# One fused recurrent-attention and feed-forward kernel: another written-out order of its steps

## The chip, the cores and the metric

The kernel runs on one core of a Trainium2 chip. The metric is the time of one execution on the device in microseconds (us); lower is better. The five engines of a core are called PE (matrix multiply; its weight loads are listed as PEld), DVE (vector), ACT (activations), POOL (general purpose) and SP, which here only issues transfers (DMAs).

## The reference

What is computed is a gated recurrent attention (an mLSTM) whose output goes through a gated feed-forward layer, all in float32:

```
q, k, v, o_gate: (4, 8, 768, 40);  i_gate, f_gate: (4, 8, 768)
for t in range(768):
    m_new = max(f[t] + m, i[t])
    C = exp(f[t] + m - m_new) * C + exp(i[t] - m_new) * outer(v[t], k[t])
    n = exp(f[t] + m - m_new) * n + exp(i[t] - m_new) * k[t]
    y[t] = sigmoid(o_gate[t]) * (C @ q[t]) / max(abs(n . q[t]), 1)
x = y as (3072, 320)
out = (sigmoid(x @ w_gate) * (x @ w_val)) @ w_out        # w_gate, w_val: 320x1536, w_out: 1536x320
```

## The kernel before

The sequence is cut into 6 chunks of 128 positions; with 4 batch entries that makes 24 units (chunk, batch entry), numbered 0 to 23, four to a chunk. Within a unit the recurrence is a masked matrix product: the scores (keys against queries) are multiplied by a matrix of decays and then applied to the values; between chunks a small state is carried.

The feed-forward layer works on whole chunks (512 rows of x). A chunk has 12 columns of blocks of the hidden width, and the first blocks are split in two halves, so that there are 103 feed-forward tiles, numbered 0 to 102; tiles 0 to 15 are chunk 0. Every product is made from a high and a low part of each operand, so a tile has 16 accumulating matmuls up (steps `t0` to `t102`, line L950), a tanh on ACT (`ta`, L963), a gate multiply on DVE (`tg`, L966), a split into a high (`th`) and a low part (`tl`, L977) and matmuls down (`p`, L988). PE, DVE, ACT and POOL each run their own instructions in the order in which they were issued.

Weights arrive in double words of 8 bytes and are decoded on the chip: for each of 30 pieces of weight, step `w..a` is an ACT operation, `w..b` three DVE operations in a row (L529, L533, L537), `w..d` the high part, `w..e` the low part (L578, L582, L584), `w..f` the load of a later piece into the freed buffer. `wg`, `wv` and `wr` are the first three pieces, `w3` to `w29` the rest. All pieces are needed by the tiles of chunk 0.

The order of all this is not computed in the kernel. It is a string, ORDER, of some 4,470 words. Each word names a list of prepared operations; each time the word comes up, the next operation of its list is issued, and `*3` issues three. A `/` issues nothing and only switches which of two PSUM buffers (the matrix unit's result memory) the next small result takes:

```
for word in ORDER.split():
    if word == "/":
        other("pa")
        continue
    key, _, n = word.partition("*")
    for _ in range(int(n or 1)):
        f, args = todo[key].pop(0)
        f(*args)
```

The opening computes units 0 and 1 by special steps. `ig`, `ih`, `iac` and `gc`, `g` are scans and small operations on the gates (DVE, L1178); `sp` spreads the gates on PE and `ex` takes the exponential on ACT; `mk` masks on POOL; `tr` transposes keys and queries on PE (L644, L647), `cp` copies them out (on DVE and ACT); `sc` makes scores on PE (L1104), `ti` multiplies them by the decays (DVE, L1109); `c0`, `c1` apply them to the values (PE, L759); `cv`, `cg`, `cr`, `cx` normalise and gate (DVE); `d0`, `d1` transpose the result on PE (L886), `dx`, `dy` write its high and low part as the feed-forward operand. Later units have `a`, `ah`, `b`, `bm`, `c`, `ci`, `cf`, `cs`, `cv`, `cg`, `cr`, `cx`, `d`, `dx`, `dy` for the same stages, and `z`, `zd`, `za`, `zm`, `zs` for the carried state. In the opening the second transposed block of unit 1 (`tr12`) takes the PSUM buffer that the scores `sc01` held, so it has to wait until `ti01` has read them. `lq`, `lk`, `lv`, `lo` and `ld` are loads issued by SP. `im` and `iq` are matmuls on zeros that keep PE at work.

Of the kernel before, what the change touches and what calls it, by code (L numbers as in the profile page):

```python
# [153 lines left out]
cv7 p16 t17*2 as8.5 t17 as8.7 t17 p15*2 t17 p15 oh1 as8.6 t17*2 cv6 t17*2 ta17 t17 p16*2 a10.0 cg6 p15*3 as8.4 t18
p16*2 cr6 aq8*2 t18*3 tg17 t18 cv7 th17 a11.0 t18*2 za6 p16 ld10 t18 ct8 o0 cx6 t18*4 p17 ah10.0 s8 p17 t18*3 tl17 e9a
p17 p15 t18 ta18 tg18 p15 d6 dx6 cg7 za7 p15 t19*3 th18 s8 t19*6 p17 t19*2 dy6 t19*3 p18 t19*2 / ci8 tl18 p17 p18 cv7
s8 cr7 ta19 s8 p18 tg19 t20*4 p17 t20*2 as9.1 t20 cf8 e8m cx7 t20 th19 as9.2 t20 tl19 t20 p19 t20*2 ah11.0 v9 t20*4
p19 p18 b8.2 p18 ta20 p19 p18 t21 tg20 t21*3 p19 bk8 th20 t21 b8.1 t21*3 bm8.2 as9.0 b8.0 t21*4 tl20 t21*2 o1 as9.3
# [1049 lines left out]
```

## Time and profile before

| | us |
|---|---|
| median of three runs | 522.29 (521.57 to 522.36) |
| the profiled execution, its time | 521.88 |
| the profiled execution, its span (first to last instruction) | 520.2 |
| around the span | 1.68 |
| PE busy | 502.3 |
| DVE busy | 318.8 |
| ACT busy | 191.1 |
| POOL busy | 156.8 |

The span is read with the engines' busy times: PE is busy for 97% of it. The mean granted clock of PE was 0.997 of full speed.

### The profile page before, as it was taken

How to read it: one execution, taken by the hardware profiler on the slowest of the kernel's cores; microseconds unless marked ns; L12 is line 12 of the kernel's file. 1: busy time of each engine (PE TensorE's matmuls, PEld its weight loads, DVE VectorE, ACT ScalarE, POOL GpSimd, SP SyncE). 2: the span in 40 equal slices, each digit the busy share in tenths (PEclk: the TensorE clock that was granted, in tenths of full speed). 3: DMA queues.
4: the chain of work that ended last, by engine and by line, in shares of the span. 5: the costliest groups of instructions: out<-in, count | busy, mean ns of one | idle time of the engine just before them, and what ended most of it. 6: DMA issues, size and time to landing. Idle time of an engine off the chain costs nothing.

```text
span 520.2 us, 13187 instructions
## 1 busy us (share of the span) xinstructions
PE 502.3 (97%) x5191; PEld 453.6 (87%) x5191; DVE 318.8 (61%) x738; ACT 191.1 (37%) x483; POOL 156.8 (30%) x207
## 2 busy tenths in 40 slices
PE   8699999999999999999999999999999999999997
PEld 7577887777899999998888888888888888999997
DVE  7899999998745657755456743847625444443322
ACT  4586667456223332233314223122323224122221
POOL 3546333445435320342402143213041321101111
PEclk9899999999999999999999999999999999999999
DMA  9777949778777995868979797498786687000000
GB/s 204 172 202 208 245 116 252 181 160 149 171 148 127 206 217 106 179 146 183 158 161 173 162 199 155 117 183 166 135 186 156 126 177 158 23 7 2 27 25 26
DMA packets 234382, 76.66 MB, mean 147 GB/s; under 512 B 213840, under 2 KB 222224, under 8 KB 234320
## 3 DMA queue, kind: packets, MB, share of 16 engines
q1 hardware_dynamic: 233232, 75.56, 67.1%
q8 instruction: 41, 0.67, 0.6%
q10 hardware_dynamic: 1088, 0.26, 0.3%
q14 instruction: 21, 0.17, 0.1%
HBM read 57.61 MB, written 17.14 MB: 144 GB/s over the span
## 4 chain that ended last, share of the span: by engine, by line
PE 82%; DVE 11%; issue 2%; ACT 1%; DMA 1%; POOL 1%; SPq 0%; DVEq 0%; POOLq 0%
PE pg L950 47%; PE po L988 23%; PE av L759 3%; PE s L781 2%; PE in L802 2%; DVE dc L537 1%; PE xt L886 1%; DVE gl L977 1%; PE s L776 1%; DVE dc L529 1%; PE av L627 1%; DMA st_o<-in_moe_w_out_dram 1%; DVE sg L966 1%; DVE xl L899 1%; DMA gin<-in_f_gate_dram 1%
## 5 line engine op out<-in xcount | busy, mean ns | idle before, releaser
L963 ACT ACTIVATE sg<-pg 128x256 f32<-128x256 f32 (+1 forms) x103 | 48.2, 468 | 231.4 <-PE pg L950 211.0
L966 DVE SCALAR_TENSOR_TENSOR sg<-sg,pg 128x256 f32<-128x256 f32 (+1 forms) x103 | 54.0, 525 | 109.3 <-ACT sg L963 65.2
L950 PE MATMUL pg<-xl,wh 128*128 128x256 f32 (+1 forms) x412 | 108.8, 330 | 0.2
L950 PE MATMUL pg<-xh,wh 128*128 128x256 f32 (+1 forms) x412 | 107.6, 333 | 1.0 <-ACT sg L963 0.6
L950 PE MATMUL pg<-xh,wl 128*128 128x256 f32 (+1 forms) x412 | 108.0, 331 | 0.0
L977 POOL TENSOR_TENSOR gl<-sg,gh 128x256 fp32r<-128x256 f32 (+1 forms) x51 | 48.8, 958 | 196.1 <-ACT gh L971 63.1
L988 PE MATMUL po<-oh,gl 128*128 128x320 f32 x288 | 88.0, 315 | 1.3 <-DVE gl L977 1.1
L988 PE MATMUL po<-oh,gh 128*128 128x320 f32 x288 | 87.9, 316 | 0.6 <-DVE gh L973 0.6
L988 PE MATMUL po<-ol,gh 128*128 128x320 f32 x288 | 88.2, 315 | 0.0
L950 PEld LDWEIGHTS pg<-xl,wh 128*128 128x128 f32 x412 | 69.8, 189 | 5.5 <-DVE xl L899 0.6
L950 PEld LDWEIGHTS pg<-xh,wh 128*128 128x128 f32 x412 | 69.2, 189 | 5.9 <-ACT sg L963 1.6
L950 PEld LDWEIGHTS pg<-xh,wl 128*128 128x128 f32 x412 | 69.3, 188 | 5.7 <-DVE wl L578 0.5
L950 PE MATMUL pg<-xl,w 128*128 128x256 f32 (+1 forms) x206 | 61.5, 335 | 0.0
L988 PEld LDWEIGHTS po<-oh,gl 128*128 128x128 f32 x288 | 53.7, 188 | 5.7 <-DVE gl L977 1.9
L988 PEld LDWEIGHTS po<-oh,gh 128*128 128x128 f32 x288 | 53.6, 188 | 5.5 <-DVE gh L973 1.3
L988 PEld LDWEIGHTS po<-ol,gh 128*128 128x128 f32 x288 | 53.7, 189 | 3.4
L950 PE MATMUL pg<-xh,w 128*128 128x256 f32 (+1 forms) x206 | 53.6, 330 | 0.0
L787 DVE TENSOR_TENSOR d<-s,d 128x384 f32<-128x384 f32 (+1 forms) x66 | 32.6, 506 | 25.9 <-PE s L781 20.8
L971 ACT ACTIVATE gh<-sg 128x256 fp32r<-128x256 f32 (+1 forms) x58 | 28.9, 498 | 48.3 <-DVE sg L966 32.6
L479 ACT ACTIVATE d<-d,at 128x128 f32<-128x128 f32 x136 | 42.7, 390 | 3.7 <-DMA d<-mscr 3.7
L977 DVE TENSOR_TENSOR gl<-sg,gh 128x256 fp32r<-128x256 f32 (+1 forms) x52 | 32.2, 619 | 14.4 <-ACT gh L971 7.0
L950 PEld LDWEIGHTS pg<-xl,w 128*128 128x128 f32 x206 | 36.6, 189 | 2.6
(151 smaller groups left out, 686.5 us busy)
## 6 DMA issues: line engine op xcount, KB each, us to landing
d<-mscr SPq DMA_DIRECT2D x22, 512.0 KB
k<-in_k_dram SPq DMA_DIRECT2D x24, 160.0 KB
v<-in_v_dram SPq DMA_DIRECT2D x24, 160.0 KB
o<-in_o_gate_dram SPq DMA_DIRECT2D x24, 160.0 KB
st_o<-in_moe_w_out_dram SPq DMA_DIRECT2D x12, 320.0 KB
scr0q<-qt SPq DMA_DIRECT2D x32, 120.0 KB
...
```

Source lines behind the costliest of these rows:

```text
L479: nc.scalar.activation(d[:, h, :], d[:, h, :], AF.Exp, bias=at[:, c, b * H + h : b * H + h + 1], scale=-1.0)
L529: nc.vector.tensor_scalar(t, t, MAX_POS, MAX_NEG, ALU.min, ALU.max)
L759: nc.tensor.matmul(dst[xs], lhs[:, xs], rhs, start=True, stop=True)
L781: nc.tensor.matmul(ps[g][:, m, :], ks[: 3 * D, h0 + m, :], qs[: 3 * D, h0 + m, :], start=True, stop=True)
L787: nc.vector.tensor_tensor(x, ps[g][:, :nh, :], x, ALU.mult)
L802: nc.tensor.matmul(pi[:, h0 : h0 + nh, :], qk[u][:r, g, :], cb[:r, b // 2, g, b % 2, : nh * DA], start=True, stop=True)
L950: nc.tensor.matmul(pg[x], w[:, a, fs] if a < 2 else w[:, fs], y[c][:, a, n0:n1], start=first, stop=a == 2 and y is xl)
L963: nc.scalar.activation(sg[0], pg[0], AF.Tanh, scale=0.5)
L966: nc.vector.scalar_tensor_tensor(sg[0], sg[0], 1.0, pg[1], ALU.add, ALU.mult)
L971: nc.scalar.activation(gh[u][:, :nt], sg[0], AF.Copy)
L977: E('gl0' if c == 0 else 'gl', f'tl{n}').tensor_tensor(gl[u][:, :nt], sg[0], gh[u][:, :nt].bitcast(F32), ALU.subtract)
L988: nc.tensor.matmul(po[t], g[c, j, t0][:, (t - t0) * P : (t - t0 + 1) * P], o[:, j, :], start=j == 0 and first, stop=j == NF - 1 and last)
```

## The change

Only the string ORDER differs. The same words stand in it, each as often as before, apart from the `/`, of which there are 43 in place of 37. So every operation, its operands, its engine and its size stay; what moves is the order in which each engine is given its instructions and SP its transfers, and which of two PSUM buffers some of the small results take. The first 165 steps follow an older sequence, and all behind them is laid anew. The first 21 words agree. Shown are the opening up to tile 0, and the stretch around tile 14 and 15:

```
     'PU': 4,
 }
 ORDER = """
-w26f w25f w29f w28f w21f iw ip*2 it if ii lq0 lk0 ib x0 x1 v1 lk1 lq1 iy ig ir x2 ig im ia gc*2 ig ih ig ih lv1 is im
-sp00 sp01 iac tr01 tr02 cp02 tr00 ex01 cp01 ex00 g wva wga cp00 wvb*2 wgb igs sc01 im tr10 tr11 v0 gc*2 cp11 lo1 sc02
-lq2 cp10 lv0 wvb wra sp10 ex10 g wgb g wgb sc00 sp11 sc11 mk01 mk00 wrb lo0 bk0 wrb*2 ti01 x4 ex11 mk11 tr12 sc10 wgd
-cp12 ti00 mk10 wvd ti02 bk1 wve ti10 c0 ie sc12 iq cv0*2 lk2 ld2 ct0 ti12 ti11 w3a z1 cv0 c1 a2.1 cg0 wrd cr0 zm1 cx0
-cv1 ct1 wge d0 w3b cv1 w3b ah2.1 w3b cv1 cg1 cr1 g w3d x3 dx0 dy0 e2 cx1 im d1 iq dx1 a2.0 w5a t0*2 dy1 t0 g lk3 t0
-ah2.0 lq3 z0 a3.0 v2 e2a t0*2 w5b*3 ah3.0 t0*3 zm0 w3f t0*2 g w5d w5e wre t0*3 wgf wrf ld3 w7a t0 ta0 a2.2 ah2.2 t0
...
-ta14 lv7 tg14 lq11 w28d aq8 e8a th14 t15 ct7 p13*3 w29b t15 tl14 t15 cf7 p13 w29b p13 t15*6 v8 p14 w28e t15*3 aq7.1
-t15*3 lv8 ta15 e7m bk7 b7.1 t15 p13*2 p14 t16 ct6 tg15 p14 lk8 t16*2 bm7.1 as9.6 zd8 t16*2 p13 e8 t16*3 p14 cs6 / b7.2
-p14 aq7.0 t16 p14 a8.1 p14 th15 lo8 t16 v7 t16*2 w29d zd6 tl15 ah8.1 w29e t16*2 p14 t16 p14 as9.5 p15 ta16 as9.7 bm7.2
...
+w26f w25f w29f w28f w21f iw ip*2 it if ii lq0 lk0 ib x0 x1 v1 lk1 lq1 iy ig v0 ig im ia ir is ig im ih igs iac ih x2
+gc sp00 gc g ex00 lv0 sp01 lo1 tr01 ig ex01 g mk00 tr02 lo0 tr00 cp01 wga mk01 cp02 sc01 cp00 wgb bk0 wva im tr10 wgb
+tr11 x4 cp10 sc02 wgb lv1 wra sp10 cp11 wvb lk2 ti01 ex10 sc00 wvb lq2 wrb sp11 wrb ex11 gc mk10 sc11 wrb ti00 tr12
+sc10 ti02 mk11 cp12 ld2 wvb wgd x3 c0 bk1 w3f ct0 ct1 sc12 cv0 cg0 wrd wge iq ti12 z1 wvd cv0 ti10 lk3 ti11 c1 wve zm1
+lq3 cv0 cr0 w3a a2.1 cx0 v2 cv1 wre cg1 d0 wgf ah2.1 cv1 w3b dx0 cv1 cr1 e2 ld3 w3b cx1 im d1 w3b gc dy0 iq w3d wrf g
+dx1 lv2 a2.0 w3e w5a dy1 w7a g t0 w5b ah2.0 t0 lq4 t0 w5b t0 e2a t0 z0 w7b g t0 a2.2 w5b w7b zm0 e2m ah2.2 gs a3.1 w5d
+lo2 t0*3 ah3.1 t0 zi t0 h0 t0*2 h0c t0*3 b2.0 ta0 w6a tg0 a3.0 w5e th0 bk2 ah3.0 e3a p0*2 t1*2 w6b t1*3 gs v5 w7b /
...
+ah7.1 w28b ta14 w28b w29b a7.0 w28d lk8 aq7.1 p13 t14 ah9.1 cs6 t15 ct6 p12 al9.1 tg14 t15*3 bk7 t15 as9.4 t15 th14
+t15 aq8 aq7.2 t15*2 ld9 tl14 za6 t15 cg6 t15 as9.7 t15 cv6 p13 aq8 t15 p13 w28e lv8 t15 v8 t15 w29b p13 as9.5 p13 w29b
+ta15 p13*2 a8.1 p13 ah7.0 p13 p14*2 w29d t15 cv6 ah8.1 t16 cv6 t16 w29e tg15 t16*2 p14 t16 p14 p13 al8.1 / ci7 th15
+p13 e8 p14 cf7 as8.6 p14 tl15 t16*2 cr6 t16 as8.5 p14 t16 a9.0 p14 t16 lo10 p14 t16*2 aq7.0 as8.4 t16 ah9.0 / b7.2
...
```

## Rows read from the trace of the kernel before

**Rows 1.** The page's part on busy time, share of the span and instructions.

```profile
PE 502.3 (97%) x5191; PEld 453.6 (87%) x5191; DVE 318.8 (61%) x738; ACT 191.1 (37%) x483; POOL 156.8 (30%) x207
```

**Rows 2.** Stretches: length, busy (instructions) by engine, PE's clock, DMA share, GB/s.

```profile
28.50:114.00 85.50, 80.50 (x856) 67.43 (x857) 81.75 (x189) 56.34 (x149) 38.65 (x45) 1.00 0.76 192
114.00:150.00 36.00, 34.56 (x405) 31.17 (x404) 25.55 (x56) 13.56 (x38) 16.91 (x23) 1.00 0.79 162
150.00:500.00 350.00, 349.12 (x3542) 321.22 (x3541) 185.22 (x427) 100.87 (x244) 86.04 (x108) 1.00 0.67 138
500.00:520.20 20.20, 16.84 (x131) 16.56 (x129) 4.56 (x12) 4.02 (x10) 2.93 (x4) 1.00 0.09 33
```

**Rows 3.** The same columns for two stretches of the opening.

```profile
10.00:20.00 10.00, 6.75 (x96) 4.85 (x94) 9.04 (x18) 7.02 (x19) 4.64 (x6) 0.95 0.99 226
20.00:30.00 10.00, 8.27 (x181) 6.76 (x174) 7.66 (x24) 7.17 (x19) 4.79 (x8) 0.88 0.59 155
```

**Rows 4.** PE's longest wait in the first 30 us: in total, times, longest.

```profile
PE pt L644 <- DVE d L1109: 2.9, 1, 2.9
```

**Rows 5.** DVE in order of time, opening: start, us, instruction, idle before it.

```profile
8.08 1.15 DVE L664 COPY kq<-pt 80x384 f32<-80x384 f32 x2 [1.77 <-PE pt L647]
...
12.95 0.15 DVE L1178 TENSOR_TENSOR mend<-gin,mg 32x1 f32<-32x1 f32 x1
13.03 0.67 DVE L537 SCALAR_TENSOR_TENSOR dc<-st,dc 128x512 int32<-128x512 int32 x1
...
14.57 0.47 DVE L1178 TENSOR_TENSOR_SCAN mg<-gin,mend 32x128 f32<-32x128 f32 x1
...
17.28 1.35 DVE L1109 TENSOR_TENSOR d<-s,d 128x384 f32<-128x384 f32 x3
```

**Rows 6.** PE in order of time, from the second unit's scores to tile 0.

```profile
14.10 0.91 PE L1104 MATMUL s<-kq 120*128 120x384 f32 x2 [0.39 <-ACT d L1084]
17.88 0.31 PE L644 MATMUL pt<-ident,k 128*80 128x128 f32 x1 [2.87 <-DVE d L1109]
...
18.24 0.81 PE L1104 MATMUL s<-kq 120*128 120x384 f32 x2
18.98 1.28 PE L759 MATMUL av<-v,d 128*32 128x41 f32 x64
...
22.33 0.88 PE L759 MATMUL av<-v,d 128*32 128x41 f32 x64
...
27.97 0.50 PE L950 MATMUL pg<-xh,wh 128*128 128x256 f32 x2
```

**Rows 7.** DVE in order of time, ahead of tile 0.

```profile
24.43 0.49 DVE L537 SCALAR_TENSOR_TENSOR dc<-st_o,dc 128x320 int32<-128x320 int32 x1
...
25.98 0.46 DVE L1178 TENSOR_TENSOR mend<-gin,mg 32x1 f32<-32x1 f32 x1
26.37 0.54 DVE L899 TENSOR_TENSOR xl<-xt,xh 128x384 fp32r<-128x384 f32 x1
26.83 0.17 DVE L869 COPY x<-x 128x64 f32<-128x64 f32 x1
```

**Rows 8.** ACT in order of time, the high part of weight piece 3.

```profile
24.96 0.47 ACT L562 ACTIVATE oh<-dc 128x320 fp32r<-128x320 f32 x1 [0.53 <-DVE dc L537]
```

**Rows 9.** DVE in order of time, around the gate multiply of tile 15.

```profile
127.12 0.69 DVE L966 SCALAR_TENSOR_TENSOR sg<-sg,pg 128x512 f32<-128x512 f32 x1 [0.34 <-PE pg L950]
...
128.60 0.79 DVE L698 STREAM_TRANSPOSE kr<-k 128x320 f32<-128x320 f32 x1
```

**Rows 10.** DVE groups by shape from 28 to 114 us: busy, mean ns, idle before.

```profile
L537 DVE SCALAR_TENSOR_TENSOR dc<-st,dc 128x512 int32<-128x512 int32 x10 | 8.4, 842 | 0.1
```

**Rows 11.** Line 537 in the whole span: min/median/max ns, first and last start.

```profile
L537 DVE SCALAR_TENSOR_TENSOR dc<-st,dc x18: 406/676/1705, 13.0 to 112.2; 128x512 int32<-128x512 int32 x12, 128x256 int32<-128x256 int32 x6
```

**Rows 12.** DVE and POOL in order of time, around 88 us.

```profile
87.71 1.71 DVE L537 SCALAR_TENSOR_TENSOR dc<-st,dc 128x512 int32<-128x512 int32 x1
...
87.58 1.29 POOL L977 TENSOR_TENSOR gl<-sg,gh 128x512 fp32r<-128x512 f32 x1 [6.87 <-ACT gh L971]
```

More of the change, by code (lines that the diff above doesn't have):

```diff
@@ L154 @@
[L154 to L158, printed above, removed]
@@ new lines @@
+lo3 p0 t2*2 w4b t2 gcs t2 e3m tg1 t2 b2.2 ah3.2 w8a p0 ct2 t2*2 w4b b3.1 bk3 bm2.2 w4d w7f t2 lk4 th1 c2 w6e w5f v3
+w8b tl1 t2 cv2 bm3.1 t2*4 cv2 ld4 t2 cg2 w4e t2 b3.0 cv2 ta2 cr2 ct3 t3 w8b t3 t2 w9a b3.2 w8b t3 w9b p1 w8d w8f t3
+bm3.2 t3*2 p1 bm3.0 w8e p1 / z2 tg2 c3 w9b th2 cx2 w9b zm2 tl2 t3 cv3 t3 w11a w9f t3 cv3 cg3 t3 d2 wvf w9d cv3 p1 p2
+cr3 w6f dx2 t3*3 w11b t3 zs1 t3 cx3 t3 p2 w11b ta3 p2 d3 w9e dy2 lk6 p1*2 dx3 tg3 p2 zs1 gc z3 th3 w12a t4 lq5 tl3 t4
+dy3 zm3 t4 p2 e4 t4 p3 w12b p3 v4 g p2 w11b / k0 t4 a4.2 t4 w13a w12b t4*2 g t4 k0c t4 ah4.2 t4 lq6 w12b t4*3 aq4.2 t4
@@ new lines @@
+dx6 ld10 t17 t18 s8 t18 tg17 t18 p16 al10.0 s8 p15 dy6 t18*2 as9.1 t18 p16 cs7 p15 s8 p15 t18 cv7 oh1 t18 za7 p15 t18
+th17 ct7 t18 o1 t18 tl17 t18*2 lk10 t18 cg7 t18 p16*2 ta18 t18 lo9 p16 oh3 p16 tg18 p17 t19*3 th18 t19*2 p17 tl18
+t19*3 a11.0 t19*3 p17 t19*2 cv7 t19 cv7 t19 p17*2 ta19 p18*3 t19 p17 t20 tg19 p18*2 cr7 p18 t20*3 th19 t20*2 tl19
+t20*3 as10.1 p19 t20*2 e10a t20 aq9 t20*3 zs7 ci8 ta20 t20 b8.1 o3 tg20 t21*2 zs7 bm8.1 t21 e10 t21 p19*2 th20 t21*2
+a10.1 aq9 t21 tl20 t21*2 as10.2 t21*4 ah10.1 t21 cf8 t21*2 al10.1 / b8.0 ta21 p20 e9 p19 bm8.0 p19 cx7 t22 as10.4 p20
@@ new lines @@
+v10 tg21 t22 p19 t22 ah11.0 t22 th21 b8.2 e9m t22*2 s9 bm8.2 t22*2 p20 aq9 p21 t22*2 zd8 as10.0 t22*3 tl21 p20 s9 t22
+p20 t22 s9 t22 d7 zd9 s9 ta22 c8 oh2 zs7 e10m tg22 dx7 ct8 dy7 as10.5 ct10 t23 v11 t23 cs8 p21 lk11 th22 t23*2 p20
+as10.7 cv8 t23 p21 cv8 tl22 t23*2 cv8 t23*4 al11.0 t23 p22 t23*4 p21 ta23 p21*2 p22 tg23 p22 t24*3 th23 as10.3 t24*4
+tl23 t24*5 p22 t24 as11.3 p23 t24*2 ci9 ta24 o2 t24 as11.0 p22 t25 tg24 t25 p22 lv10 t25 a11.1 t25 th24 t25*4 tl24 t25
+cf9 t25 aq10 t25*2 cg8 t25 ld11 t25*3 cr8 p23 as10.6 ta25 p23 p24 ah11.1 p23 tg25 aq10 p23*2 bk9 t26 lq15 th25 t26*3
@@ new lines @@
+t39*5 e13a t39 aq12 t39*3 s12 t39*3 s12 t39*3 s12 / d10 ta39 aq12 c11 dx10 as13.1 lo12 cs11 t40 p37 tg39 lk14 t40*3
+th39 t40*3 tl39 t40*3 cv11 t40 dy10 t40*2 p38 za11 p38*2 cg11 t40*2 p39 t40 ta40 p39*2 p38 tg40 p38 t41*2 a15.0 t41
+th40 t41*2 p38 t41 cv11 t41 tl40 t41 cv11 t41*2 cr11 t41*2 zs9 p40 v15 t41 cx11 t41*2 d11 ld14 ta41 t41 p39*2 tg41
+aq12 p39 t42*2 oh7 t42*3 th41 t42 o7 t42*2 oh6 p40 tl41 zs9 t42 dx11 t42*2 p40 e13 p41 dy11 t42 aq13 p40 p41 t42 aq13
+t42*3 aq13 p40 ta42 p40 b12.0 as13.4 tg42 b12.2 p41 bm12.0 zs11 t43 th42 t43*2 ct14 t43*2 tl42 t43 ah15.0 t43 lv15
@@ new lines @@
+a14.1 t43*4 al15.0 o6 t43*2 p42 t43*2 p42 p41 ta43 p41 p42 e14 b12.1 t43 p41 s13 t44 tg43 p42 s13 t44*2 ah14.1 t44 s13
+t44 bm12.1 t44 al14.1 t44 s13 t44*3 zs11 t44*2 th43 t44*3 tl43 t44 p42 as14.5 / ci12 ta44 lo13 p43 p42 tg44 p43*2
+a14.0 p43 th44 p43*2 ct12 t45*2 bm12.2 t45*3 tl44 t45*3 ah14.0 t45*3 al14.0 t45*3 p44 t45*2 e13m c12 ta45 tg45 cf12
+th45 zd13 t46 lk15 cs12 t46 zd12 t46 as14.3 t46*2 as14.0 t46 ci13 as15.1 t46 cf13 t46 p44 tl45 p44 lv14 p44 t46 cv12*2
+t46 cv12 t46 cg12 as14.1 t46 p45 cr12 t46*2 as14.7 bk13 t46*2 as14.2 ta46 p44 p45 p44 / b13.0 e14a p45 as14.4 t47
@@ new lines @@
+ah16.1 p47*2 t49 p48*2 tg49 t50*3 cv13 th49 p48 t50 dx12 t50*2 cr13 t50 as15.6 t50 al16.1 t50 dy12 t50 p48 as15.7 p48
+tl49 p48 p49 t50 aq15 t50 as16.5 t50*2 as16.4 t50 zd14 p49*2 ta50 zd15 aq15 / b14.2 t50 lo15 bm14.2 p48 p49 tg50 p48
+b14.0 p48 t51 th50 b14.1 t51 e16a s15 bm14.1 t51*2 s15 bm14.0 t51 s15 t51 cx13 t51 lo16 e16 tl50 p49 / d13 zs13 c14
+dx13 e16m s15 dy13 lq18 t51 a16.0 p50*2 p49 bk16 p49 p50 p49*2 zs13 ah16.0 p50 v18 t51*6 ld18 t51 p49 zs13 ci14 ta51
+ct15 t51 p50 p49 tg51 p50*2 t52*2 th51 t52 al16.0 t52*2 cf14 t52 as16.2 t52 cs14 t52 as16.6 p49 t52 za14 as16.7 p50
@@ new lines @@
+tl51 t52*2 lk17 cg14 p51 t52*4 p50 t52 as16.0 zd16 ta52 / ci15 lq21 p51*2 cf15 t53*2 cv14 tg52 p50 as17.3 p50*2 p51
+cv14 t53 th52 cv14 t53 as16.3 cr14 / b15.2 t53*2 as16.1 t53 b15.1 p51*2 bm15.1 p51*2 t53 tl52 t53 / b15.0 bm15.2 p51
+t53 s16 cx14 bm15.0 t53 lv16 p51*2 t53 as17.1 t53*3 p52 d14 ta53 c15 e18 cs15 t53 lk18 p52 cv15 za15 p52 zs13 p52 cv15
+cg15 p52*2 t54 cv15 p52 cr15 s16 t54 p52 s16 tg53 p51 cx15 t54 s16 v19 t54*2 zs15 th53 t54 / d15 tl53 t54 aq16 dx15
+t54 aq16 t54 dx14 t54 aq16 t54 a18.0 p52 as17.0 t54*2 ld17 t54 ah18.0 t54 a17.1 p53 al18.0 p53 ta54 p52*2 p53 dy14
@@ new lines @@
+e18a tg57 t58*3 p55 p56 p55 t58 p55*3 t58 as18.7 th57 t58 za16 t58 tl57 cf16 t58 p56 a19.0 t58*4 ah19.0 t58 cs16 p57
+lv17 p57 t58*3 lk19 ta58 p56*2 p57*2 ct17 p57 tg58 p57 ct16 aq18 p56*3 aq18 p57 th58 t59 lv18 t59 cv16 tl58 cv16 t59
+cg16 aq18 t59 p57*2 t59*2 e18m t59 p58*2 p57 t59*2 zd18 p58*2 t59 / b17.0 t59 bm17.0 t59*2 al19.0 t59*2 cv16 as19.1
+p58 cr16 p58 ta59 t59 as18.5 p57 cx16 / b17.1 ct18 tg59 as18.6 p58*2 t60 as18.4 t60 th59 b17.2 t60 o11 e19 p57 p58
+zs15 t60 tl59 t60*2 lq20 bm17.1 t60 e19a t60 bm17.2 lo19 p58*2 a19.1 t60 s18 t60*2 e19m t60*3 p58 t60*2 ta60 ci17 tg60
@@ new lines @@
+as22.7 b20.1 p67 tg68 ld22 p67 t69 p67 lv20 oh15 t69 th68 p67 bm20.1 zs19 t69*2 tl68 bm20.0 t69*2 oh14 t69 p67 a23.0
+p68 t69*3 a22.0 t69*3 ah23.0 t69 ah22.0 p68 a23.1 p68 al22.0 p67 t69 p67 p68 ta69 t69 al23.0 as22.1 p67*2 p68 tg69
+as22.2 p68*3 zs19 t70 p67 t70 th69 t70 as22.5 / b20.2 t70 e22a t70 as22.0 p69 t70 o15 t70 p68 lo21 e22 p67 p68 ci20
+tl69 zs19 p68 t70 as22.3 t70*2 e22m s21 t70 s21 t70*2 s21 t70 s21 t70 p68 lo22 t70 ta70 p69*2 o14 p69 ct20 p69 tg70
+aq21 p69 ct21 p69 t71 aq22 t71 th70 t71 lv21 t71 tl70 t71*2 bm20.2 t71*2 ah23.1 t71 cf20 al23.1 t71*6 p69 p70 ta71
@@ new lines @@
+as22.6 p70 p69 p70*2 t71 c20 tg71 t72 cs20 p69*2 t72 cv20 th71 t72 cv20 cg20 p69 t72 as23.2 t72 tl71 t72 lv23 t72 cv20
+t72 as22.4 cr20 t72*2 as23.5 p70 t72 p70 ld23 p70 t72*2 lo23 t72*2 aq22 p71 b21.2 ta72 as23.3 p70*2 bm21.2 p71 b21.0
+p71 b21.1 bm21.0 t73 bm21.1 s22 t72 p70 s22 p70 tg72 t73 lv22 t73*2 th72 t73*3 ct22 as23.4 t73*3 p70 zs19 p71*2 tl72
+p71 ci21 as23.1 p71 t73 cf21 p71*2 cx20 t73*4 d20 ta73 s22 c21 s22 dx20 as23.0 e23a t74 cs21 t74 p71 p72 t74*2 t73
+p71*2 tg73 p72*3 t74 dy20 th73 t74*3 tl73 t74*4 p72 t74*3 p73 t74 aq23 ta74 p73 p72 aq22 p73 e23 p73 tg74 p73 aq23
@@ new lines @@
+t84*3 cg23 t84 th83 t84*2 cv23 t84*2 tl83 t84*3 p83 t84*4 p82 p83 ta84 t84 p83 p82 tg84 p82 t85*2 dy22 t85 th84 t85*4
+tl84 t85*8 p84*2 ta85 p83*2 t85 p84 t86 tg85 t86*2 p83 cv23 t86 th85 t86*4 tl85 t86*2 cr23 t86*5 p84*2 ta86 p84 p85*2
+t86 t87*2 tg86 t87*4 th86 p85 t87 cx23 t87 tl86 t87*8 p85 ta87 p85 p86 p85 tg87 p86 t88*3 th87 p86 t88*2 tl87 t88*5
+p86 t88*3 p87 t88*3 p87 ta88 p86*2 d23 tg88 t89*2 th88 t89*3 tl88 t89*10 p87 p88 ta89 p88 t89 dx23 p87*2 tg89 p87 t90
+dy23 t90*2 th89 t90*3 tl89 t90*9 p88 p89 ta90 t90 p89 p88 tg90 p88 t91 p89 th90 t91*4 p88 t91*2 tl90 t91*8 p90 p89
@@ new lines @@
+ta91 p89*2 t91 p90*2 tg91 t92*4 th91 p90 t92 oh20 t92 tl91 t92*3 o20 t92 p90 t92*6 p90 ta92 p91*3 tg92 p91 t93*3 th92
+t93*4 tl92 t93*8 p91*2 ta93 p92 t93 oh21 p92*2 tg93 t94*2 o21 t94*2 th93 t94*4 tl93 t94*7 p92*2 ta94 p93*3 t94 t95 p92
+tg94 t95*4 th94 t95*3 tl94 t95*7 p94 p93 ta95 p93 t95 p94*2 tg95 t96*4 th95 t96*4 p93 p94 t96 tl95 t96*6 p95*2 ta96
+p94*2 t96 p95 t97 tg96 t97*4 th96 t97*4 tl96 t97*2 p95 t97*4 p95 t97 ta97 p96*3 tg97 p95 t98*3 th97 t98*4 tl97 t98*9
+p96 ta98 p96*2 p97 tg98 p97 t99*3 th98 t99*4 tl98 t99*8 p97*2 ta99 p97*2 t99 p98 t100 tg99 t100*4 th99 t100*3 tl99
@@ L256 @@
+t100*8 p98 ta100 p98*3 tg100 p98 t101*3 th100 t101*2 tl100 t101*10 p99*2 ta101 p99*2 t101 p99 t102 tg101 t102*4 th101
+t102 p99 t102*2 tl101 t102*8 p100 ta102 p100*3 tg102 p100*2 p101 th102 p101*2 tl102 p101*3 p102*5 oh22 p102 oh23 o22
+o23
 """
```

195 lines of the change are left out of this document (72 added, 123 removed).

## The prediction

> **What bounds the kernel now.** I read the page's busy times first. PE is busy for 502.3 of 520.2 us [rows 1], and the change alters no instruction, so nearly all there is to win is PE's idle time, some 18 us, and to lose there is whatever new waiting an order makes. Next I read busy time by stretch. From 150 to 500 us PE lacks 0.88 us of 350, and in the last 20.2 us it lacks 3.4 [rows 2]: the last words, the down matmuls of the last two tiles and the stores, are the same in both orders but for a place or two, and for the rest no order can give much. From 28.5 to 114 us the picture is another: DVE is busy for 81.75 of 85.5 us and PE for 80.5 [rows 2]. There the vector engine, which decodes all weights while it also serves the attention, sets the pace, and PE takes what is left. What remains is the opening ahead of tile 0, which begins at 27.97 us [rows 6]. PE's longest wait of the run lies in it: 2.9 us in front of a transpose, for DVE at L1109 [rows 4, 6]. DVE itself stands still for 1.77 us before 8.08, waiting for PE's transposes [rows 5]. And the granted clock of PE is 0.95 and 0.88 of full in 10 to 20 and 20 to 30 us [rows 3], where it is 1.00 in all later stretches [rows 2], so for a part of that time PE ran at the lower of its two levels; the first matmul group of unit 0 then takes 1.28 us and its twin of unit 1, later, 0.88 [rows 6].
>
> So three questions decide: how much sooner tile 0 begins, how much of that the vector-bound stretch keeps, and whether the new order behind 114 us makes PE wait.
>
> **Until c0.** In the new order ti01 stands directly behind the first operation of wvb, ahead of two more of wvb, three of wrb and one gate scan; now it stands behind all of these. The transpose tr12 needs only the buffer that ti01 reads, so its wait of 2.87 us [rows 6] should go. What is late next is DVE: c0 needs the three products of unit 0, which end at 17.28 + 1.35 = 18.63 us [rows 5]. Two things bring them forward. The pair of gc operations and g's scan and subtraction now stand behind iac and ahead of the copies cp01 and cp02, and they need nothing of PE, so they fill the 1.77 us in which DVE waits for the transposes. And three operations that stand ahead of the products now go behind them: one gate update of 0.15 us, the last decode step of the second weight piece, 0.67, and a scan of 0.47 [rows 5], together 1.29. That makes 1.77 + 1.29 = 3.06, or 15.6 us for the end of the products. PE's own chain is then the later one: the scores sc11 wait for ACT's exponentials and stay near 14.1; with their 0.8 us, the transposes (17.88 to 18.24: 0.36) and sc10 (18.24 to 18.98: 0.74) [rows 6] PE is free for c0 at about 16.0. I take 16.4, for the hand-overs between four engines: 18.98 - 16.4 = 2.6 us earlier. The bounds are 1.3 (the 1.77 us are not filled) and 3.0 (PE's chain alone).
>
> **From c0 to c1.** Now 22.33 - 18.98 = 3.35 us [rows 6]. In the new order the product ti10, 0.55 us (as one of the three of [rows 5] is longer than 0.45), moves behind c0, but DVE has idle time there, and with PE at full clock c0 itself may take 0.88 instead of 1.28. I take no change, bounds 0.4 either way.
>
> **From c1 to tile 0.** Now 27.97 - 22.33 = 5.64 us [rows 6]. The way goes over unit 1's normalisation to its last copy cx1 at 26.83. The third decode step of piece 3, 0.49, a gate operation, 0.46, and the low part dy0, 0.54 [rows 7], stand ahead of cx1 and move behind it: 1.49 less. Against that, the high part of piece 3, 0.47 on ACT [rows 8], moves ahead of dx1, which tile 0 needs, and it must wait for that third decode step: 0.49 + 0.47 = 0.96 more. Net 0.5 earlier; bounds 0 and 1.5.
>
> The sum to tile 0 is 2.6 + 0 + 0.5 = 3.1 us earlier, with 0.9 and 4.9 as the ends. SP's transfers are reordered too: the gate's store moves in front of the third weight piece, the values of unit 0 move up, those of unit 1 go behind the first piece of w_out, and the load w3f stands before the loads of unit 3 and waits there for the third piece's decode. In 10 to 20 us the DMA engines are 0.99 busy, in 20 to 30 us 0.59 [rows 3]. Within the first stretch transfers of like size change places, and what c0 needs comes sooner; I cost it at nothing, and if unit 1's values came late, c1 would wait, which is inside the bounds above.
>
> **The vector-bound stretch.** I added up, for each tile, the DVE durations of this profile over all steps that stand ahead of the tile's gate multiply, in the old order and in the new. The new order has more work in front of tile 5 (3.2 us), tile 6 (2.5) and tile 9 (2.9), the same at tile 10, less at tile 12 (1.35), the same at tile 13, and more at tile 15. There it is cs6, three of cv6, cg6 and za6, all of unit 6, and the transpose a8.1 of 0.79 us that go in front, 2.56 in all, while a9.0 and cf7, 1.30, go behind: net 1.26. With the multiply at 127.12 [rows 9] PE is from there on nearly without idle time, so what is late here stays late. Of the extra work at tiles 5 to 9 most is paid back by tile 12. I take 1.3 us given back; the ends are 0 (from 114 to 150 us DVE is busy for 25.55 of 36 us [rows 2], so it may have room) and 2.9 (the surplus at tile 9, in the stretch without room).
>
> **Behind that.** The 103 tiles keep between their last matmul up and the next tile's first the same few filling matmuls on the average, and PE's idle time there is 0.88 us in 350 [rows 2]. Nothing gained, nothing lost; bounds 0.9 either way.
>
> The sum is -3.1 + 1.3 + 0 = -1.8 us. It stands against the profiled execution: span 520.2 to 518.4, time 521.88 to 520.1. The median of the three runs is 0.41 above that execution, so I predict 520.5.
>
> **Rivals.** First, nothing is kept (chance 0.25). The surplus of 2.9 us at tile 9 is worked off while PE stands still, and PE cannot catch up because it has its own full load of 80.5 in 85.5 us [rows 2]: -3.1 + 2.9 = -0.2, 522.1 us. For it speaks that DVE has only 3.75 us of slack in that stretch; against it, that PE has 5 us of its own. A low clock at another place gives the same: from 10 to 30 us PE loses 0.05 and 0.12 of 10 us [rows 3], 1.7 in all, and should PE wait before tile 0 in the new order, that falls on tile 0's matmuls.
>
> Second, more is kept (0.18): the 1.3 us at tile 15 are covered by DVE's room behind 114 us, and a fifth of the 6.4 us that PE idles between 28.5 and 150 us [rows 2] goes as well. -3.1 - 1.3 = -4.4, 517.9 us.
>
> Third, slower (0.15): the two engines that work side by side block each other more often. The wide third decode step takes 842 ns on the average from 28 to 114 us [rows 10], the line's median is 676 [rows 11], and the longest, 1.71 us at 87.71, began just after a POOL subtraction at 87.58 of 1.29 [rows 12]. Ten such steps pay 10 x 0.166 = 1.7 us; were all 81.75 us of DVE work swollen like that (a fifth), it would be some 16 us. The new order lays other POOL steps beside other DVE steps in the stretch that DVE bounds; a quarter more of the 16 is 4 us, and -1.8 + 4 = +2.2, 524.5 us. It makes the kernel slower from 2.8 us more on. For it speaks that these are the largest stretched durations of the run; against it, that both orders put equal work side by side. The Trainium skill, "SBUF — State Buffer", section "Who interferes with whom", says that DVE and GpSimd share one pair of ports under an exclusive lock, so that the later of two such instructions stands still until the earlier is done; the row at 87.71 agrees. By that rule the price depends on which instruction starts first, which an order changes.
>
> **How the numbers follow.** My forecast has chance 0.42, with a range of its own of 519.3 to 521.5. A measurement of this kernel can tell about 0.2%, 1.04 us, from no change. Faster by more: 0.38 of the forecast, the second rival's 0.18 and 0.03 of the first, 0.59. Within 0.2%: 0.04 and 0.21, 0.25. Slower: the third's 0.15 and 0.01 of the first, 0.16. The range that leaves out 2 in 10 reaches from the second rival to near the third: 517.9 to 524.0.
>
> **What would show it.** Right: no wait of PE over 1 us in front of a transpose between 14 and 18 us; DVE without its 1.8 us gap at 7 us; c0 near 16.4, tile 0 near 24.9, tile 15's gate multiply 1 to 3 us earlier than 127.12, and then a constant lead. It is wrong if tile 0 begins no earlier than 27, if DVE's mean durations from 28 to 114 us differ, or if PE idles over 2 us more behind 114 us.

## The result and the profile after

The changed kernel takes 510.48 us (median of four runs, 509.88 to 511.05); the kernel before took 522.33 beside it (521.57 to 522.73). The ratio is 0.9775, 95% interval 0.9758 to 0.9792: 11.85 us faster, where 1.8 were forecast, and outside the range of 517.9 to 524.0. The profiled execution took 509.88, its span is 508.2.

The page's busy times, to be read against [rows 1]:

```profile
PE 500.9 (99%) x5191; PEld 455.0 (90%) x5191; DVE 303.7 (60%) x738; ACT 189.3 (37%) x483; POOL 152.7 (30%) x207
```

PE's idle time fell from 17.9 to 7.3 us. The row that speaks loudest is DVE's: the same 738 instructions, shape for shape, are busy for 15.1 us less. Stretches after, against [rows 2, 3] (length, busy time and instructions of PE, PEld, DVE, ACT, POOL, PE's granted clock, DMA share, GB/s):

```profile
10.00:20.00 10.00, 9.28 (x199) 7.14 (x197) 8.29 (x22) 8.31 (x22) 5.08 (x7) 1.00 1.05 229
20.00:30.00 10.00, 8.65 (x102) 6.79 (x90) 7.43 (x25) 8.24 (x22) 6.19 (x9) 1.00 1.06 255
28.50:114.00 85.50, 84.90 (x936) 71.80 (x935) 79.73 (x199) 56.79 (x155) 38.74 (x50) 1.00 0.85 203
114.00:150.00 36.00, 36.00 (x449) 34.78 (x447) 20.66 (x53) 13.82 (x35) 19.80 (x27) 1.00 0.86 179
150.00:500.00 350.00, 350.00 (x3464) 322.50 (x3463) 179.05 (x420) 97.97 (x240) 79.78 (x100) 1.00 0.64 132
```

In the opening the clock is at its upper level throughout. From 28.5 to 114 us PE lacks 0.6 us instead of 5.0: DVE gets 199 instructions done in 79.73 us there, where it did 189 in 81.75. From 114 to 500 us PE has no gap left. The opening on PE, against [rows 4, 6] (start, us, instruction, idle before it; the change shifts lines by 9, so L759 is now L768 and L950 is L959):

```profile
13.58 0.91 PE L1113 MATMUL s<-kq 120*128 120x384 f32 x2 [0.23 <-ACT kq L675]
...
15.42 0.28 PE L653 MATMUL pt<-ident,k 128*80 128x128 f32 x1
...
16.49 0.82 PE L768 MATMUL av<-v,d 128*32 128x41 f32 x64
19.06 1.11 PE L768 MATMUL av<-v,d 128*32 128x41 f32 x64 [0.47 <-DVE d L1118]
...
24.03 0.49 PE L959 MATMUL pg<-xh,wh 128*128 128x256 f32 x2
```

The wait in front of `tr12` (the row at 15.42) is gone, c0 begins at 16.49 and tile 0 at 24.03. On DVE, against [rows 5, 9]: the gap ahead of the copies has shrunk from 1.77 to 0.51 us, the last products that c0 needs end at 15.42 instead of 18.63, and the gate multiply of tile 15 is 10.7 us earlier.

```profile
8.93 1.19 DVE L673 COPY kq<-pt 120x512 f32<-120x512 f32 x2 [0.51 <-PE pt L656]
14.53 0.89 DVE L1118 TENSOR_TENSOR d<-s,d 128x384 f32<-128x384 f32 x2
...
116.39 0.69 DVE L975 SCALAR_TENSOR_TENSOR sg<-sg,pg 128x512 f32<-128x512 f32 x1
```

So the lead is 3.9 us at tile 0, 10.7 at tile 15 and 12.0 at the end of the span. The forecast has the first of these nearly right; what it lacks arises between tile 0 and tile 15.

**Where DVE's time went.** Each instruction of one trace was set beside the same step of the other. A step's quiet duration is the median over both traces of that kind and shape with no POOL instruction beside it; what an instruction takes above that is called stretching here. Between the start of tile 0 and the gate multiply of tile 15 (sums over DVE's instructions; neighbouring records overlap, by 12 us in all, so that the parts add up to more than the length):

```
                 tile 0    tg15   length   quiet  stretching   idle
before            27.97  127.12    99.15   89.85       14.50   6.50
after             24.03  116.39    92.36   91.33        5.63   7.77
after - before    -3.94  -10.73    -6.79   +1.48       -8.87  +1.27
```

The new order does 1.5 us more of DVE's work in this stretch, and it is 6.8 us shorter, because the work is stretched by 8.9 us less. Read on PE, the 6.8 us are 4.8 us less idle time (5.86 before, 1.10 after) and 2.0 us less busy time (93.29 and 91.26). Of the 15.1 us that DVE is busy less in the whole run, some 1.5 fall in the opening and some 4.8 behind tile 15, where PE sets the pace and they win little. The stretching lies in one kind of meeting only. Of DVE's instructions in the stretch, those that begin while a POOL instruction is running and that have their operands in SBUF alone carry 14.72 of it before (32 of them) and 5.93 after (31). Those that read PSUM (39 and 53 begin beside a running POOL instruction) carry 0.02 and -0.16, those during which POOL begins -0.01 and -0.11. Such meetings in the trace of before, POOL and then DVE:

```profile
72.10 0.87 POOL L584 TENSOR_TENSOR ol<-dc,oh 128x320 fp32r<-128x320 f32 x1 [2.31 <-ACT oh L562]
72.93 1.09 POOL L500 TENSOR_SCALAR_AFFINE_SELECT d<-d 128x1024 f32<-128x1024 f32 x1
73.99 0.90 POOL L819 TENSOR_TENSOR cst<-cst,cdec 128x164 f32<-128x164 f32 x1
74.85 0.66 POOL L671 TENSOR_TENSOR kq<-qc,rmask 80x256 f32<-80x256 f32 x1
...
72.62 0.55 DVE L787 TENSOR_TENSOR d<-s,d 128x384 f32<-128x384 f32 x1
73.09 1.47 DVE L1178 TENSOR_TENSOR gin<-mend,mg 32x512 f32<-32x512 f32 x1
74.49 0.55 DVE L529 TENSOR_SCALAR dc<-dc 128x256 f32<-128x256 f32 x1
75.07 0.59 DVE L533 TENSOR_SCALAR dc<-dc 128x256 int32<-128x256 int32 x1
```

The gate operation at 73.09 begins 0.16 us behind POOL's mask, which has 0.93 us to go; it takes 1.47 us where it takes 0.67 alone, 0.80 more. No idle time is shown: the wait is inside the duration, and the page counts it as busy. The score multiply at 72.62, which reads PSUM, takes its usual 0.55 beside POOL's 0.87. Over the stretch such a wait comes to the rest of the POOL instruction less some 0.14 us: these rests sum to 19.5 us in the 32 meetings before and 10.7 in the 31 after. The new order has as many meetings, but POOL's instructions have less left to run in them. The third decode step of [rows 10, 11, 12], at its worst 1.71 us, is at its worst 0.96 now (from 28 to 114 us: line, times, shortest/median/longest ns), and the mean of its wide form fell from 842 to 710 ns (as in [rows 10]):

```profile
L546 DVE SCALAR_TENSOR_TENSOR dc<-st,dc x14: 387/676/955, 31.1 to 103.9; 128x512 int32<-128x512 int32 x9, 128x256 int32<-128x256 int32 x5
...
L546 DVE SCALAR_TENSOR_TENSOR dc<-st,dc 128x512 int32<-128x512 int32 x9 | 6.3, 710 | 0.0
```

### The profile page after: what moved, and what is told of

The parts are those of the page before. It is cut to its first block, busy times and chain, and to the rows that moved or that the text cites. A ratio compares the mean times of both kernels' runs of the same rounds, so it can differ in the third digit from the quotient of the medians.

```text
span 508.2 us, 13186 instructions
## 1 busy us (share of the span) xinstructions
PE 500.9 (99%) x5191; PEld 455.0 (90%) x5191; DVE 303.7 (60%) x738; ACT 189.3 (37%) x483; POOL 152.7 (30%) x207
## 4 chain that ended last, share of the span: by engine, by line
PE 95%; DVE 2%; ACT 2%; issue 1%; DVEq 0%
PE pg L959 54%; PE po L997 25%; PE av L768 3%; PE in L811 3%; PE s L790 2%; PE s L785 2%; PE xt L895 1%; PE av L636 1%; PE pwarm0x L1060 1%; ACT d L488 1%; PE s L1113 1%; PE pt L653 1%; PE pt L656 1%; ACT dc L533 0%; PE mb L1088 0%
## 5 line engine op out<-in xcount | busy, mean ns | idle before, releaser
L959 PE MATMUL pg<-xh,wh 128*128 128x256 f32 (+1 forms) x412 | 111.3, 336 | 0.0
L959 PE MATMUL pg<-xh,wl 128*128 128x256 f32 (+1 forms) x412 | 108.6, 330 | 0.0
L959 PE MATMUL pg<-xl,wh 128*128 128x256 f32 (+1 forms) x412 | 107.4, 329 | 0.1
L997 PE MATMUL po<-ol,gh 128*128 128x320 f32 x288 | 87.0, 313 | 0.0
L959 PEld LDWEIGHTS pg<-xl,wh 128*128 128x128 f32 x412 | 69.6, 188 | 5.0 <-DVE xl L908 0.3
L959 PEld LDWEIGHTS pg<-xh,wh 128*128 128x128 f32 x412 | 69.5, 188 | 4.8 <-DVE sg L975 0.4
L959 PEld LDWEIGHTS pg<-xh,wl 128*128 128x128 f32 x412 | 69.4, 188 | 4.8
L959 PE MATMUL pg<-xl,w 128*128 128x256 f32 (+1 forms) x206 | 63.1, 333 | 0.0
L959 PE MATMUL pg<-xh,w 128*128 128x256 f32 (+1 forms) x206 | 53.5, 329 | 0.0
L959 PEld LDWEIGHTS pg<-xl,w 128*128 128x128 f32 x206 | 37.2, 188 | 2.3
L959 PEld LDWEIGHTS pg<-xh,w 128*128 128x128 f32 x206 | 35.0, 188 | 2.9
```

The costliest lines, as they stand in the source:

```text
L959: nc.tensor.matmul(pg[x], w[:, a, fs] if a < 2 else w[:, fs], y[c][:, a, n0:n1], start=first, stop=a == 2 and y is xl)
L997: nc.tensor.matmul(po[t], g[c, j, t0][:, (t - t0) * P : (t - t0 + 1) * P], o[:, j, :], start=j == 0 and first, stop=j == NF - 1 and last)
```

## The experiments

The first question is where the gain lies. In e1 and e2 theory A says that the opening is the cause of nearly all of it; theory B says that it is the stretch from tile 0 to tile 16, to which the opening adds its own few microseconds. The second question is why the stretch is shorter. Theory B says: fewer microseconds in which DVE stands behind POOL. Its rival C is that the new order only puts the right steps ahead, with the stretching a by-product. In o1 and k1 theory A is another one, named there.

**Where the gain lies.** Four orders made of the two, each word issued as often as before, the `/` apart (`||` marks the seam; in e3 and e4 some words that the other order has earlier stand just ahead of it):

```
e1  order of after, first 165 words   ... t0 lq4 t0 w5b t0 e2a || ie g z0 a3.0 t0 t0 ...   rest as in before
e2  order of before, first 150 words  ... t0 t0 dy1 t0 g || w3f lk3 lq3 v2 wre wgf ...     rest as in after
e3  order of after up to tile 17      ... / bm7.0 || t17 p14 p14 t17 th16 ...              rest as in before
e4  order of before up to tile 17     ... p15 p14 p15 oh0 || t17 p14 as9.0 p15 ...         rest as in after
```

> The new order's first 165 words, all others in the old order. Theory A (the opening is the cause: the vector engine gets ahead by the 3.9 us that tile 0 starts earlier, and the rest follows from that): most of the 11.8 us, a time of 511 to 515 us. Theory B (the cause is the stretch from tile 0 to tile 16, where vector instructions that start while a POOL instruction runs are stretched, by 14.7 us in all in the old order and 5.8 in the new): tile 0 starts near 24 us, but at most those 3.9 us are kept, 518 to 522 us, and the vector engine's busy time stays near 319 us instead of falling to 304.

> The old order's first 150 words, all others in the new order. Theory A (opening): 519 to 522 us. Theory B (the stretch behind it, by how vector and POOL instructions meet): tile 0 starts near 28 us, vector busy time near 305 us, 513 to 516 us.

> The new order up to the first matmul of tile 17, all others in the old order. Both theories: 510 to 513 us. A rival (the new order is also better where the matrix engine bounds, behind tile 16): 516 to 520 us.

> The old order up to the first matmul of tile 17, all others in the new order. Both theories: 521 to 523 us, no change. The rival (the new order gains behind tile 16): 514 to 518 us.

Measured, with before at 522.41 us beside them:

```
                     median    ratio, 95% interval       tile 0    tg15   stretching  idle
e1 new opening       518.43    0.9919 (0.9894-0.9944)     23.15  123.03        13.69  7.77
e2 old opening       514.95    0.9855 (0.9837-0.9874)     28.49  121.47         5.38  8.58
e3 new to tile 16    511.27    0.9781 (0.9765-0.9798)     23.35  116.61         5.64  8.57
e4 old to tile 16    523.86    1.0030 (1.0016-1.0045)     28.55  128.40        14.27  7.22
```

The opening alone brings 4.0 us, everything behind it alone 7.5; together that is 11.4, and the new order up to tile 16 brings 11.1. e1, e2 and e3 came out in theory B's ranges, and the opening as the cause of nearly all (511 to 515 for e1) is out; DVE is busy for 314.8 us in e1 and for 305.2 in e2; e4 came out 0.9 above its range. e1 keeps most of its lead: 4.8 us at tile 0, 4.1 at tile 15, 4.2 at the end of the span. These places are good to some 0.9 us: e1, e3 and after have the same words up to tile 0, which begins at 23.15, 23.35 and 24.03. The stretching belongs to the words between tile 0 and tile 16, whichever opening stands ahead of them. One row of e1 and one of e2 show the stretch that DVE bounds: with the new opening it looks as in [rows 2], with the old opening as after.

```profile
28.50:114.00 85.50, 80.78 (x819) 66.96 (x818) 80.07 (x185) 54.58 (x146) 37.04 (x44) 1.00 0.76 193
```

```profile
28.50:114.00 85.50, 84.95 (x874) 71.91 (x873) 77.62 (x194) 58.84 (x159) 38.59 (x49) 0.98 0.80 201
```

Behind tile 16 there is a little: from 150 to 500 us PE is busy for 350.00 us in after and e2, 349.24 and 349.19 in e1 and e3, which have the old words there. That is 0.8 us, too little to see between the medians of e3 and after, whose intervals overlap. e4 is slower than before by 1.5 us. Its profiled execution, the slowest of its ten executions, lags by 0.6 us at tile 0 and 1.3 at tile 15, where its words are those of before, and by 4.0 at the end. Behind the seam PE has a wait that neither before nor after has, by the profile for a load of the output gate:

```profile
151.09 0.52 PE L788 MATMUL s<-qs,ks 120*128 120x128 f32 x3 [1.95 <-DMA o<-in_o_gate_dram]
```

So the seam itself can cost something, and e4 doesn't show what the new words alone would do there; a gain behind tile 16 it doesn't show.

**What stretches DVE.** The rule that the prediction cites goes on in the same place (the Trainium skill, "SBUF — State Buffer", section "Who interferes with whom"): a vector instruction with two SBUF inputs meets only a GpSimd instruction that reads SBUF, one with at most one SBUF input meets none outside the two-port modes. The rows above agree for readers of PSUM. So each of POOL's 73 low-part subtractions was replaced by two memsets, which read nothing; c1 has the order of before, c2 that of after. Both leave out POOL's low parts of weights and tiles. Other things change with it: a pair of memsets is 15 to 24% shorter than its subtraction and comes in two pieces, and it waits for no data. The edit, shortened (the subtraction stands in four places):

```
-  eng.tensor_tensor(dst, x, high, ALU.subtract)
+  if eng is nc.gpsimd:
+      for _ in range(2):
+          eng.memset(dst.bitcast(F32), 0.0)
+  else:
+      eng.tensor_tensor(dst, x, high, ALU.subtract)
```

> The kernel before, where POOL's subtractions for the low parts of weights and gated products (73 steps) are each two memsets to zero of the same tile: POOL stays at work for about as long, but reads nothing. The low parts that POOL made are left out of the result. Theory B (vector instructions on SBUF alone stand still behind a running POOL instruction that uses the same memory): from tile 0 to tile 15 these subtractions stand in front of 7.1 of the 14.7 us of stretching, so vector busy time falls by 5 to 8 us and the time to 515 to 519 us. Rival C (the old order's loss is a matter of waits between engines, and the long vector instructions are only a symptom): vector busy time as before, 521 to 523 us.

> The same edit in the kernel after. Theory B: these subtractions stand in front of only 3.3 of 5.9 us here, and the matrix engine already bounds the stretch, so 508.5 to 510.5 us and the distance between the two orders shrinks from 11.9 to 6 to 9 us. Rival C: both change by the same amount within 1 us.

c1 takes 516.26 us, ratio 0.9892 (0.9864 to 0.9920) to before at 521.93; c2 takes 512.76, 0.9830 (0.9800 to 0.9859). In c1 stretching falls from 14.50 to 9.29 and the stretch from 99.15 to 94.67 us, with DVE's idle time unchanged (6.50 and 6.56): theory B as expected. As the edit also shortens and shifts POOL's work, the time alone doesn't show that the reads are the reason. The meetings inside c1 do: 14 DVE steps with two inputs in SBUF begin behind a memset, with 2.66 us of it to go in all, and carry 0.0 us of stretching; 8 such steps behind POOL instructions that read, with 5.37 us to go, carry 4.26. The 14 decode steps with one input (TENSOR_SCALAR) that begin behind a memset, with 3.61 us to go, do carry 1.96; by the rule they would have to run in a two-port mode, which no row here shows. Both kinds behind one run of memsets in c1; alone the two take 0.32 and 0.48 us:

```profile
61.30 1.43 POOL L578 MEMSET ol<- 128x320 f32 x3
...
61.45 0.56 DVE L529 TENSOR_SCALAR dc<-dc 128x320 f32<-128x320 f32 x1
61.93 0.47 DVE L769 TENSOR_TENSOR k<-k,d 128x320 f32<-128x320 f32 x1
```

The place shown before, in c1, POOL and then DVE:

```profile
72.57 0.82 POOL L678 TENSOR_TENSOR kq<-qc,rmask 120x384 f32<-120x384 f32 x1
...
72.61 1.33 DVE L1185 TENSOR_TENSOR gin<-mend,mg 32x512 f32<-32x512 f32 x1
73.87 0.27 DVE L529 TENSOR_SCALAR dc<-dc 128x256 f32<-128x256 f32 x1
74.18 0.29 DVE L533 TENSOR_SCALAR dc<-dc 128x256 int32<-128x256 int32 x1
```

The decode steps take 0.27 and 0.29 with POOL idle, against 0.55 and 0.59; the gate operation has a new partner, which still reads SBUF, and takes 1.33. c2 missed: 512.76, where 508.5 to 510.5 was expected. Its stretching is 5.04, a little less than after's 5.63, but DVE's idle time rose from 7.77 to 11.35 us. POOL no longer waits for its data and runs in places up to 10 us ahead of where it stands in after; that the hand-overs which the order was laid for no longer fit would explain the idle time, but wasn't tested. DVE's own busy time is as in after (304.0 and 303.7). Taken together, the two orders, 11.9 us apart, are 3.5 apart without these reads: the old order gains 5.7 us by it and the new one loses 2.3 (before's own median was 0.4 lower beside c1 and c2 than beside after).

**The same steps in two halves.** Here nothing is left out: 22 of POOL's masks and 65 of its 73 low parts (not those of `wr`) are cut in two instructions, so that behind these DVE finds at most half a step to wait for. The edit, shortened:

```
-  nc.gpsimd.affine_select(out=d, in_=d, pattern=[[0, H], [1, L]], ...)
+  for h in range(0, H, 4):
+      nc.gpsimd.affine_select(out=d[:, h : h + 4, :], in_=d[:, h : h + 4, :], pattern=[[0, 4], [1, L]], ...)
-  eng.tensor_tensor(dst, x, high, ALU.subtract)
+  for cs in (first half of the columns, second half):
+      eng.tensor_tensor(dst[cs], x[cs], high[cs], ALU.subtract)
```

> Order of before; each decay mask, each low part of a weight and each tile's low part that POOL computes is cut into two instructions over half the elements. Nothing is left out. Theory B (a vector instruction on SBUF alone that begins behind a running POOL instruction stands still until that one is done): it now waits for the rest of a half. Those three kinds of step carry 11.1 of the 14.7 us of stretching between tile 0 and tile 15, and the waits of 0.7 to 1.1 us shrink to under 0.6: stretching 8 to 11 us, vector engine busy 312 to 316 instead of 318.8, time 517 to 520. Rival C (what counts is only which steps stand ahead of which; the stretching is a loss of rate while both engines run): POOL has the same elements to do and more instructions, so nothing is won: 521.5 to 523.5, stretching 14 or more.

> The same cut in two, in the order of after. Theory B: these three kinds carry 3.85 of only 5.8 us of stretching there, mostly short remainders already: stretching 4 to 5 us, and the stretch up to tile 15 is no longer bound by the vector engine, so 510 to 511.5, no change against after. Rival C: none either, or a loss as in f1 of up to 1 us.

f1 (order of before) takes 521.20, ratio 0.9971 (0.9961 to 0.9982) to before at 522.56; f2 (order of after) 510.78, 0.9775 (0.9760 to 0.9789). f2 is after's time, as both theories allow. In f1 stretching fell to 11.48 and DVE's busy time to 312.0, nearly and fully as theory B had it, and C's "14 or more" is out; but the time missed B's 517 to 520. The stretch is only 0.9 us shorter: 3.0 less stretching, but DVE's idle time rose from 6.50 to 8.55, and POOL, with 87 more instructions, is busy for 172.3 us instead of 156.8. The idle time grew in front of first decode steps, which wait for ACT (from 0.7 to 2.3 us), and by 0.5 us in front of a step that waits for a mask of POOL's; and ACT's own step there waits for a low part of POOL's, 3.7 us in all where it was 2.2 before (in total, times, longest):

```profile
ACT dc L525 <- POOL ol L581: 3.7, 3, 2.5
```

The opening of f1 is also 0.8 us longer, at a granted clock of 0.82 from 10 to 20 us and 0.84 from 20 to 30. So what DVE stood less was lost again, as POOL's results came later, and the one run that cuts the stretching of the old order with order and work as they were gained only 1.4 us of time.

**Is the stretch bound by DVE?** d1 (order of before) and d2 (order of after) leave out the first of the three decode steps, the clamp:

```
-  nc.vector.tensor_scalar(t, t, MAX_POS, MAX_NEG, ALU.min, ALU.max)
```

> The kernel before without the first of the three vector decode steps of every piece of weight (the clamp of the exponent, left out of the computation), some 11 us of vector work between 28 and 114 us and 1.9 us before; where POOL and vector instructions meet may shift, but nothing is done against it. If the vector engine bounds that stretch, as theory B says, the time falls by 6 to 11 us, to 511 to 516 us. If the matrix engine or waits bound it, by less than 3 us.

> The same edit in the kernel after, whose matrix engine idles for only 0.6 us between 28.5 and 150 us: theory B says that the vector engine no longer bounds it, so the time falls by no more than the 1 to 2 us that the opening may give, to 508 to 510 us. If the vector engine still bounds it, 500 to 505 us.

d1 takes 516.92, 0.9906 (0.9883 to 0.9929), 5.0 us less than before, between its two forecasts (6 to 11 us if DVE bounds, under 3 if not); d2 takes 509.44, 0.9752 (0.9735 to 0.9770), 1.0 us less than after. From tile 0 to tile 15, 9.1 us of quiet DVE work less shorten the stretch by 3.8 us in the old order and by 0.3 in the new. In before DVE sets the pace there, but only as far as PE has idle time to give back: 5.86 us of it in before, 2.89 left in d1, while DVE's own idle time nearly doubled, and 1.10 in after. There PE sets the pace, and this is why c2 and f2 have nothing more to win.

**What in the opening.** o1 takes the order of before and moves four words, so that `ti01` reads its buffer early; k1 puts eight matmuls on zeros ahead of `tr12`, so that PE's clock stays up.

```
o1
- lq2 cp10 lv0 wvb wra sp10 ex10 g wgb g wgb sc00 sp11 sc11 mk01 mk00 wrb lo0 bk0 wrb*2 ti01 x4 ex11 mk11 tr12 sc10 wgd
+ lq2 cp10 lv0 mk01 mk00 bk0 ti01 wvb wra sp10 ex10 g wgb g wgb sc00 sp11 sc11 wrb lo0 wrb*2 x4 ex11 mk11 tr12 sc10 wgd
k1
- ... x4 ex11 mk11 tr12 sc10 wgd
+ ... x4 ex11 mk11 ik*8 tr12 sc10 wgd
```

> Order of before with four words (mk01, mk00, bk0, ti01) moved ahead of the third operation of wvb. Theory A (the opening's gain comes from the transpose tr12, which waits 2.9 us for the buffer that ti01 reads): that wait falls under 1 us, c0 begins 1.3 to 2.6 us earlier than 18.98, tile 0 by 1 to 2 us, time 520 to 521.5. Rival: the buffer's wait covers another one (the products of unit 0 on the vector engine end at 18.6 anyway): c0 within 0.5 us of 18.98 and 522 or more.

> Order of before with eight matmuls on zeros put ahead of tr12, where PE stands still for 2.9 us. Theory A (the stall costs the wait itself; the low granted clock is a small part): clock 0.95 and 0.88 from 10 to 30 us become 1.00, the matmul group c0 takes 0.9 instead of 1.28 us, and the time falls by 0 to 0.8 us: 521.3 to 522.3. Rival (the clock is most of the opening's 4.0 us): 519.5 or less.

o1 takes 521.47, 0.9985 (0.9975 to 0.9995); k1 523.26, 1.0016 (1.0000 to 1.0032). In o1 `tr12` runs at 14.88 without a wait, and the 2.9 us turn up one group later, in front of c0. The row names POOL's step on `k`, but that one ended at 18.09; the last of unit 0's products on DVE begin only at 18.29:

```profile
14.88 0.27 PE L644 MATMUL pt<-ident,k 128*80 128x128 f32 x1
...
18.93 1.12 PE L759 MATMUL av<-v,d 128*32 128x41 f32 x64 [2.92 <-POOL k L762]
...
18.29 1.34 DVE L1109 TENSOR_TENSOR d<-s,d 128x384 f32<-128x384 f32 x3
```

By the place of c0 (18.93) the rival holds; its time, 522 or more, was not met, and o1's lies at the upper end of theory A's range. The wait of [rows 4] alone is worth 0.8 us by the ratio (0.3 to 1.3), and DVE's queue ahead of the products, which the new opening shortens, is what holds c0. In k1 the clock is 1.00 from 10 to 20 us and the matmuls of c0 take 0.82 us in place of 1.28, but the fillers, 0.49 us each, end 1.1 us behind the wait that they were to fill, and tile 0 begins at 28.68. From c0 to c1 (21.98) it is 1.4 us shorter than before, 1.92 for 3.35, but from c0 to tile 0 only 0.4, 8.62 for 8.99:

```profile
18.67 0.49 PE L1065 MATMUL pfill7x<-warm 128*128 128x128 f32 x2
19.00 0.27 PE L644 MATMUL pt<-ident,k 128*80 128x128 f32 x1
...
20.06 0.82 PE L759 MATMUL av<-v,d 128*32 128x41 f32 x64
```

The time, 523.26, is above theory A's 521.3 to 522.3. The rival that the clock is most of the opening's gain is out by these 0.4 us; how much a shorter filling would have given wasn't tried.

## Why the prediction was wrong

- **Until c0** (-2.6): 2.49 us. Right, and for its reasons: the gap on DVE filled but for 0.51 us, `tr12` without its wait, the products done at 15.42 where 15.6 was worked out, and, as the text said and o1 shows, DVE late next.
- **c0 to c1** (no change, 0.4 either way): 2.57 us in place of 3.35, so 0.8 was won, outside the 0.4. The prediction named the faster c0 at full clock and the moved product, and put both at nothing. At full clock not c0 alone but all four groups from c0 on are shorter: c1 could have begun after 2.10 us, and waits 0.47 for a product on DVE (the row at 19.06).
- **c1 to tile 0** (-0.5): 4.97 in place of 5.64, 0.7 less. The sum to tile 0 is 3.94 for 3.1, inside its ends, and e1 shows that such a lead is kept but for 0.6 us.
- **The vector-bound stretch** (+1.3 given back): this is the step that failed. The count of work was right, +1.48 us of quiet duration for +1.26. The durations were not: "I added up, for each tile, the DVE durations of this profile" takes each step with the wait that it had in the old order, as if it were its own. 14.5 us of those durations were waits behind POOL, which belong to the order, and the new order has 8.9 less of them. The stretch gained 6.8 where 1.3 was to be lost. The prediction's own sign of being wrong came true here: DVE's mean durations from 28 to 114 us differ (842 and 710 ns for the wide third decode step).
- **Behind that** (0, 0.9 either way): from tile 15 to the end of the span the lead grew by 1.3 us, a little over the bound. PE's 0.88 us of idle time from 150 to 500 us went; in the medians of e3 and after it can't be told from nothing.
- **The third rival** had the mechanism and its place, with the rule of the Trainium skill ("SBUF — State Buffer", section "Who interferes with whom") that the later instruction stands still, and nearly its size, "some 16 us" of swelling in all, where 14.5 were measured. The size was luck: it spreads one form's excess over all DVE work, while in the trace 32 of some 207 instructions carry it. It was given one sign: "a quarter more of the 16". An order can as well take it away, and it took 60% of it. The rival that more is kept took a fifth of the 6.4 us that PE idles between 28.5 and 150 us, where nearly all went (0.6 is left), and did not ask what made DVE slow.
- **The bounds**: had that rival been open to the other side with half of its 16 us, the range would have begun at 520.5 - 8 = 512.5, and still 2 us above the result.

What stays open is why the new order's meetings are shorter, whether by a rule of whoever laid it out or by its start times as they fell; no order was run that moves POOL's or DVE's steps alone. That the 8.9 us less stretching made the stretch shorter rests on the sum above, in which nothing else of DVE's time shrank, and on c1 and d1, where less DVE time in the old order shortened the stretch; c1 changed more than the reads, and f1, the cleanest cut, gave its gain back as idle time. No run took away all 8.9 us and left the rest as it was.
